# Loading all gate and value weights in the first gate step, and placing a finished block four raw blocks back

## The chip, the cores and the metric

The kernel runs on one core of a Trainium2 chip. The metric is the time of one launch in device microseconds, as the median of repeated runs. One more execution was taken under the hardware profiler, and all rows below come from it.

## The reference, cut to what matters

```python
# q, k, v: (8 batches, 8 heads, 576, 64), fp32
k_p = k.reshape(B, H, 72, 8, 64).mean(axis=3); v_p = likewise
scores = (q @ k_p.T) / 8;  attn = softmax(scores);  o = attn @ v_p
x = o.transpose(0, 2, 1, 3).reshape(4608, 512)
h = (sigmoid(x @ w_gate) * (x @ w_val)) @ w_out       # 512 -> 1536 -> 512
y = (h @ w_in); out = (y * cos(y)) @ w2_out           # 512 -> 2048 -> 512
```

The weights come as eight-byte doubles (the kernel reads them as pairs of 32-bit words), everything else as fp32.

## The kernel before, in words

The 4608 rows are worked through in nine chunks of 512 rows. Attention, the two gate products and the first half of the second layer are interleaved so that TensorE always has the next product to run. A chunk c of the gate stage has twelve gate steps f = 0 to 11. A gate step multiplies the chunk's xT (a high and a low fp32r part) by one 128-column block of w_gate and one of w_val (`gv_step`, L591; three products for each of four k-blocks, 24 matmuls, L601 to L603). ScalarE then takes the sigmoid of the gate product into `g` (L608), VectorE multiplies it by the value product (L609), and a task sent to the next step stores it to DRAM (`gd<-g`, L613). Beside each gate step stand pieces of the next chunk's attention: transposing q (`q_step`, L462/L464), scores and softmax (`s_step`, L475 to L492 and `normal`), transposing the probabilities (`a_step`, L563 to L567), the product with v (`x_step`, L584 to L586), and pooling k and v on GpSimd (L362). In chunk 0 the steps 0 to 2 run as halves of 256 columns, the first halves ahead of the loop.

The weights are converted once, in chunk 0, just ahead of the gate steps that use them. There are 24 blocks, n = 2f for the gate block of step f and n = 2f+1 for its value block. A block goes through five stages:

- a load of 512 KB into a raw tile (`load`, L116, issued on SyncE's queue at L124);
- an exponent stage on ScalarE (`stage_exponent`, L143);
- two bit stages on VectorE (`stage_bits`, L148 and L153);
- the high part on ScalarE (`stage_high`, L161), written to the finished block's own place;
- the low part on VectorE (`stage_low`, through the helper at L66), written to the second half of that place.

`split` (L300) moves this chain on by one round each gate step: first the low parts of blocks whose high part is made, then the high parts of blocks whose bits are done, then exponents of up to four raw blocks that are loaded, then the bits of two. Each engine executes its instructions strictly in this order. A PE matmul of step f needs both parts of blocks 2f and 2f+1.

28 slots w0 to w27 hold both kinds of tile. Finished block n goes to slot n, raw block n to slot n + AHEAD, so block n overwrites raw block n - AHEAD, and its high part waits for the low part of block n - AHEAD, the last reader of that raw tile. From chunk 1 on slots w24 to w27 serve the conversion of the later weights.

SyncE issues every DMA of the kernel, in program order, and waits for whatever the next one needs. Eight raw blocks are loaded before the loop; in the loop each gate step of chunk 0 loads two more at its start (L1243 to L1245), which stand behind the store of the previous step's `g`.

PSUM has two rings of four banks: tag g for gate and value products (two steps deep), tag t for everything of the attention.

Of the kernel before, what the change touches and what calls it, by code (L numbers as in the profile page):

```python
# [23 lines left out]
def attention_two_mlps(  # L24
# [33 lines left out]
    NF = FF // P  # L58
# [46 lines left out]
        "g": (w_gate, True), "v": (w_val, True), "o": (w_out, False),  # L105
        "i2": (w2_in, True), "o2": (w2_out, False),
    }
    AHEAD = 2
    NSLOT = 28
    order = [(kind, f) for f in range(NF) for kind in "gv"]  # L110
    slots = [(wp, f"w{n}") for n in range(NSLOT)]
# [1 line left out]
    raws, blocks = [], {}  # L113
    done = {"exponent": 0, "bits": 0, "high": 0, "parts": 0}

    def load(slot=None, item=None):  # L116

        kind, f = item or order[len(raws)]
        pool, tag = slot or slots[len(raws) + AHEAD]
        t = pool.tile([P, 512], I64, tag=tag, name=f"raw_{kind}{f}")  # L120
        w, columns = sources[kind]
        c = slice(f * P, (f + 1) * P)
        if columns:
            nc.sync.dma_start(  # L124
                t.rearrange("p (kb c) -> p kb c", kb=KB), w[:, c].rearrange("(kb p) c -> p kb c", p=P)
            )
        else:
            nc.sync.dma_start(t, w[c, :])
        if item is None:
            raws.append(t)  # L130
        return t

    def load_all():
        while len(raws) < min(len(order), len(slots) - AHEAD):
            load()
# [38 lines left out]
    def far_stores():  # L174
        while ready:
            nc.sync.dma_start(*ready.pop(0))
# [83 lines left out]
    def i2_weights(hold):  # L260

        made = {}

        def begin(n, j):
            raw = hold[:, n % 4]
            nc.sync.dma_start(
                raw.rearrange("p (kb c) -> p kb c", kb=KB),
                w2_in[:, j * P:(j + 1) * P].rearrange("(kb p) c -> p kb c", p=P),
            )

        def convert(n):
            stage_exponent(hold[:, n % 4])
            stage_bits([hold[:, n % 4]])

        def high(n, j):
            tag = free_i2.pop(0)
            t = wp.tile([P, 2, DM], F32R, tag=tag, name=f"wi2{j}")
            nc.scalar.copy(t[:, 0], words(hold[:, n % 4], F32, 1))
            made[j] = t
            place["i2", j] = wp, tag  # L280

        def low(n, j):
            t = made.pop(j)
            split_lo(nc.vector, t[:, 1], words(hold[:, n % 4], F32, 1), t[:, 0])
            blocks["i2", j] = t

        events = {}
        for n, j in enumerate(PAIRED):
            at = n if n < 4 else 11 + 5 * (n - 4) // 4
            for later, fn, args in (  # L290
                (4, low, (n, j)), (0, begin, (n, j)), (2, convert, (n,)), (3, high, (n, j)),
            ):
                events.setdefault(at + later, []).append((fn, args))
        order_ = {low: 0, high: 1, convert: 2, begin: 3}
        for n in range(max(events) + 1):
            for fn, args in sorted(events.get(n, ()), key=lambda e: order_[e[0]]):
                fn(*args)
            yield

    def split(upto=None, n=2):  # L300

        upto = len(raws) if upto is None else upto
        while done["parts"] < done["high"]:
            stage_low(done["parts"])
            done["parts"] += 1
        while done["high"] < done["bits"]:
            stage_high(done["high"])
            done["high"] += 1
        while done["exponent"] < min(done["bits"] + 2 * n, upto):
            stage_exponent(done["exponent"])  # L310
            done["exponent"] += 1
        some = range(done["bits"], min(done["bits"] + n, done["exponent"]))
        stage_bits(some)
        done["bits"] += len(some)
# [3 lines left out]
    def refill(tag):  # L318
        if not refills:
            free_i2.append(tag)  # L320
            return
        kind, j = refills.pop(0)
        t = wp.tile([P, 2, DM], F32R, tag=tag, name=f"w{kind}{j}")
        nc.sync.dma_start(t.bitcast(F32), wd[kind, j])
        blocks[kind, j] = t
        place[kind, j] = wp, tag
# [264 lines left out]
    def gv_step(c, f, half=None):  # L591
        cols = slice(0, C) if half is None else slice(half * C // 2, (half + 1) * C // 2)
        n = cols.stop - cols.start
        x = xT[c][..., cols]
        pg = []
        for kind in "gv":
            w = block(kind, f)
            p = bank("g", [P, n], f"p{kind}{c}_{f}_{cols.start}")
            for kb in range(KB):
                wh, wl = (w[:, n, kb * P:(kb + 1) * P] for n in range(2))  # L600
                nc.tensor.matmul(p, wh, x[:, 0, kb], start=kb == 0, stop=False)  # L601
                nc.tensor.matmul(p, wh, x[:, 1, kb], start=False, stop=False)  # L602
                nc.tensor.matmul(p, wl, x[:, 0, kb], start=False, stop=kb == KB - 1)  # L603
            pg.append(p)
        g = halves.pop(f, None)
        if g is None:
            g = gv.tile([P, C], F32, tag="g", name=f"g{c}_{f}", bufs=4)
        nc.scalar.activation(g[:, cols], pg[0], AF.Sigmoid)  # L608
        nc.vector.tensor_tensor(out=g[:, cols], in0=pg[1], in1=g[:, cols], op=ALU.mult)  # L609
        if half == 0:  # L610
            halves[f] = g
        elif c == 0:
            afterwards(1, lambda: nc.sync.dma_start(gd[f], g))  # L613
        elif f < HF:
            firsts[c, f] = g
            afterwards(1, lambda: nc.sync.dma_start(od[c][0, :, f], g[:, :HALF]))
        else:
            folded(c, f - HF, firsts.pop((c, f - HF)), g)
# [8 lines left out]
    def tick():  # L627
        clock[0] += 1
        for fn in tasks.pop((clock[0], False), ()):
            fn()  # L630

    def tock():
        for fn in tasks.pop((clock[0], True), ()):
            fn()
# [492 lines left out]
    with tc.manual_schedule():  # L1127
# [84 lines left out]
        def far_step():  # L1212
            far_stores()
            next(far, None)

        plans = [plan(c) for c in range(1, NC)]
        for c in range(NC):
            last = c == NC - 1
            beside = [[] for _ in range(NF)]
            if not last:  # L1220
                steps, early = plans[c]
                for n in range(NF):
                    if c == 0:
                        beside[n] += early[n]
                    beside[n] += steps[n]
                    if c + 1 < NC - 1:
                        beside[n] += plans[c + 1][1][n]
            else:
                far_stores()
                for _ in far:  # L1230
                    far_stores()
                far_stores()
                free_i2.extend(f"w{n}" for n in range(2 * NF, NSLOT))
                at.release()
                mp = tc.alloc_tile_pool(name="mp", bufs=1, side="left", reuse_waits="tile")
                i2 = i2_weights(
                    mp.tile([P, 4, 512], I64, tag="x2", name="raw_i2", bufs=2)
                )
                pp[0] = tc.alloc_tile_pool(name="pp1", bufs=1, side="left", reuse_waits="tile")
            for at_f, f in enumerate(FOLDED if c else range(NF)):  # L1240
                tick()
                if c == 0:
                    for _ in range(2):  # L1243
                        if len(raws) < 2 * NF:
                            load()  # L1245
                    split()
                elif last:
                    if at_f == NF - 1:
                        pp[0].release()
                        pp[0] = tc.alloc_tile_pool(  # L1250
                            name="pp2", bufs=1, side="left", reuse_waits="tile"
                        )
                    (unit_go if at_f == NF - 1 else go.go)()
                    next(i2)
                else:
                    split()
                    far_step()
                gv_step(c, f, 1 if c == 0 and f < FIRST else None)
                if last:
                    for kind in "gv":  # L1260
                        refill(place[kind, f][1])
                    next(i2)
                    for n in range((0, 0, 0, 1, 1, 1, 2, 2, 2, 2, 1, 0)[at_f]):
                        if n:
                            go.go()
                        o_next()
                    if at_f == NF - 1:
                        unit_go()
                elif c:
                    far_step()  # L1270
                for step in beside[at_f]:
                    step()
                tock()
        while tasks:
            tick()
# [107 lines left out]
```

## Time and profile before

| | |
|---|---|
| median of 3 runs | 1812.24 us (1810.19 to 1814.11) |
| the profiled execution | 1815.71 us, its span 1813.9 us |
| PE busy | 1759.1 us, 97% of the span |
| DVE busy | 1117.2 us, 62% |
| ACT busy | 913.9 us, 50% |
| DMA, mean | 219 GB/s |

The page cuts the span into 40 slices of 45 us. PE is the busy engine in nearly all of them; the exceptions lie at the start. A wait of another engine costs time only where PE runs dry because of it. Windows give, for a stretch, the busy time of each engine, the granted TensorE clock (1.00 is 2.4 GHz, 0.50 is 1.2 GHz) and the share of DMA time.

### The profile page before, as it was taken

The numbers are of one execution on the slowest core, as the hardware profiler recorded it, in microseconds if no ns is written. First come the engines' busy times: TensorE is split into PE (matmuls) and PEld (weight loads), VectorE is DVE, ScalarE is ACT, GpSimd is POOL, SyncE is SP. The second block draws the span as 40 slices with busy tenths as digits, with TensorE's granted clock in tenths as the row PEclk, the third lists the DMA queues.
The fourth block names the chain that finished last, engine by engine and source line by source line (L and its number), as shares of the span: only waits on it lengthen the run. The fifth ranks groups of instructions, "written<-read, shape, count | busy, mean of one in ns | idle before, by whom it ended". The sixth has DMA issues, their size and how long they took to land. (4 is left out here: it accounts for less than half of the span.)

```text
span 1813.9 us, 24656 instructions
## 1 busy us (share of the span) xinstructions
PE 1759.1 (97%) x8560; PEld 1474.6 (81%) x8560; DVE 1117.2 (62%) x1830; ACT 913.9 (50%) x1528; POOL 535.4 (30%) x656
## 2 busy tenths in 40 slices
PE   5879999999999999998999999999999999999999
PEld 4768888888888888886888888888887878888887
DVE  7675656546565655345666776776676665565665
ACT  6463544445454444335555555555555554444443
POOL 4102454644454422210003333443334440000000
PEclk8889999999999999999999999999999999999999
DMA  8434475666556754957877778778738798666664
GB/s 235 143 104 139 146 222 177 223 187 191 174 194 211 225 186 164 367 191 232 280 261 259 255 245 263 253 251 260 259 131 275 239 323 277 211 218 217 210 218 148
DMA packets 291741, 397.49 MB, mean 219 GB/s; under 512 B 54560, under 2 KB 231200, under 8 KB 291616
## 3 DMA queue, kind: packets, MB, share of 16 engines
q1 hardware_dynamic: 291616, 395.91, 67.0%
q8 instruction: 68, 1.11, 0.3%
q14 instruction: 57, 0.47, 0.1%
HBM read 242.22 MB, written 153.62 MB: 218 GB/s over the span
## 5 line engine op out<-in xcount | busy, mean ns | idle before, releaser
L609 DVE TENSOR_TENSOR g<-pv,g 128x512 f32<-128x512 f32 (+1 forms) x111 | 75.0, 676 | 280.7 <-issue 130.4
L904 PE MATMUL ph<-x,wi 128*128 128x512 f32 x576 | 224.5, 390 | 0.4 <-DVE r L920 0.4
L905 PE MATMUL ph<-x,wi 128*128 128x512 f32 x576 | 224.2, 389 | 0.0
L906 PE MATMUL ph<-x,wi 128*128 128x512 f32 x576 | 224.1, 389 | 0.0
L910 DVE SCALAR_TENSOR_TENSOR r<-n,ph 128x512 f32<-128x512 int32 x144 | 98.8, 686 | 198.4 <-issue 91.3
L916 ACT ACTIVATE r<-r 128x512 f32<-128x512 f32 x144 | 91.1, 633 | 237.2 <-DVE r L913 107.2
L938 POOL TENSOR_TENSOR s<-r,r 128x256 f32<-128x256 f32 x64 | 75.2, 1175 | 442.4 <-DVE r L920 324.3
L601 PE MATMUL pg<-xT,wg 128*128 128x512 f32 (+1 forms) x444 | 180.5, 406 | 2.3 <-ACT e L519 2.3
L66 DVE TENSOR_TENSOR sp<-sf,sp 128x1024 fp32r<-128x1024 f32 x112 | 132.7, 1227 | 81.0 <-ACT sp L994 81.0
L603 PE MATMUL pg<-xT,wg 128*128 128x512 f32 (+1 forms) x444 | 173.6, 391 | 1.1 <-DVE wg L66 1.1
L602 PE MATMUL pg<-xT,wg 128*128 128x512 f32 (+1 forms) x444 | 173.4, 391 | 0.1
L603 PE MATMUL pv<-xT,wv 128*128 128x512 f32 (+1 forms) x444 | 171.1, 385 | 0.0
L601 PE MATMUL pv<-xT,wv 128*128 128x512 f32 (+1 forms) x444 | 171.1, 385 | 0.0
L602 PE MATMUL pv<-xT,wv 128*128 128x512 f32 (+1 forms) x444 | 171.0, 385 | 0.0
L994 ACT CAST sp<-sf 128x1024 fp32r<-128x1024 f32 x112 | 112.4, 1055 | 67.6 <-PE py_B L1097 25.0
L608 ACT ACTIVATE g<-pg 128x512 f32<-128x512 f32 (+1 forms) x111 | 65.2, 587 | 135.7 <-PE pg L603 83.5
L904 PEld LDWEIGHTS ph<-x,wi 128*128 128x128 f32 x576 | 108.4, 188 | 23.6 <-DVE r L920 1.1
L905 PEld LDWEIGHTS ph<-x,wi 128*128 128x128 f32 x576 | 108.3, 188 | 22.6
L906 PEld LDWEIGHTS ph<-x,wi 128*128 128x128 f32 x576 | 108.2, 188 | 22.5
L1092 PE MATMUL py_A<-tc,sp 128*128 128x512 f32 x384 | 120.6, 395 | 0.0
L913 DVE SCALAR_TENSOR_TENSOR r<-n,r 128x512 f32<-128x512 int32 x144 | 108.3, 752 | 5.0
L66 DVE TENSOR_TENSOR up<-uf,up 128x1024 fp32r<-128x1024 f32 x84 | 102.3, 1218 | 5.4 <-ACT up L818 5.4
(178 smaller groups left out, 4086.0 us busy)
## 6 DMA issues: line engine op xcount, KB each, us to landing
sf<-sd SPq DMA_DIRECT2D x112, 512.0 KB
so<-so SPq DMA_DIRECT2D x84, 512.0 KB
uf<-od SPq DMA_DIRECT2D x168, 256.0 KB
sd<-s SPq DMA_DIRECT2D x64, 512.0 KB
wo<-wo SPq DMA_DIRECT2D x56, 512.0 KB
od<-tg SPq DMA_DIRECT2D x48, 512.0 KB
sd<-r SPq DMA_DIRECT2D x64, 256.0 KB
raw_o<-in_moe_w_out_dram SPq DMA_DIRECT2D x28, 512.0 KB
```

Source lines behind the costliest of these rows:

```text
L66: engine.tensor_tensor(out=lo, in0=x, in1=hi.bitcast(F32), op=ALU.subtract)
L601: nc.tensor.matmul(p, wh, x[:, 0, kb], start=kb == 0, stop=False)
L602: nc.tensor.matmul(p, wh, x[:, 1, kb], start=False, stop=False)
L603: nc.tensor.matmul(p, wl, x[:, 0, kb], start=False, stop=kb == KB - 1)
L904: nc.tensor.matmul(p, wh, x[kb][:, 0], start=kb == 0, stop=False)
L905: nc.tensor.matmul(p, wh, x[kb][:, 1], start=False, stop=False)
L906: nc.tensor.matmul(p, wl, x[kb][:, 0], start=False, stop=kb == KB - 1)
L910: nc.vector.scalar_tensor_tensor(out=r, in0=n, scalar=-C1, in1=p, op0=ALU.mult, op1=ALU.add)
L913: nc.vector.scalar_tensor_tensor(out=r, in0=n, scalar=-C2, in1=r, op0=ALU.mult, op1=ALU.add)
L916: nc.scalar.activation(r, r, AF.Sin, scale=0.5)
L994: nc.scalar.copy(t[:, 0, h * w:(h + 1) * w], got[c, n, h])
L1092: nc.tensor.matmul(p, x[:, 0, m, s], w, start=fresh and m == 0, stop=False, skip_group_check=True,)
```

## The change

Two edits. AHEAD becomes 4: raw block n goes to slot n + 4 and finished block n takes the place of raw block n - 4 (slots w4 to w27 for the 24 raw blocks, all of them fresh). And the two loads at the start of each gate step of chunk 0 go; instead `load_all` issues all that are missing, sixteen, at the end of gate step 0.

```diff
-    AHEAD = 2
+    AHEAD = 4
...
                 if c == 0:
-                    for _ in range(2):
-                        if len(raws) < 2 * NF:
-                            load()
                     split()
...
                 for step in beside[at_f]:
                     step()
+                if c == 0 and at_f == 0:
+                    load_all()
                 tock()
```

`load_all` (L133) loads until `min(len(order), len(slots) - AHEAD)` = 24 blocks are there. As `split` looks at how many blocks are loaded, the conversions move too: step 0 finds no ninth and tenth block, and from step 1 on each round works on blocks two numbers lower than before.

On SyncE's queue, from the last load of the next chunk's keys to the store of step 2. Before:

```order
L380 DMA raw_k_2_655<-in_k_dram 64x1x512
L613 DMA gd<-g_0_463 128x512
L124 DMA raw_g_665<-in_moe_w_gate_dram 128x4x128
L124 DMA raw_v_667<-in_moe_w_val_dram 128x4x128
L613 DMA gd<-g_1_517 128x512
L124 DMA raw_g_741<-in_moe_w_gate_dram 128x4x128
L124 DMA raw_v_743<-in_moe_w_val_dram 128x4x128
L454 DMA q_256_785<-in_q_dram 128x8x64
L613 DMA gd<-g_2_600 128x512
```

The same place now, from the end of the batch of sixteen:

```order
L124 DMA raw_v_680<-in_moe_w_val_dram 128x4x128
L124 DMA raw_g_682<-in_moe_w_gate_dram 128x4x128
L124 DMA raw_v_684<-in_moe_w_val_dram 128x4x128
L613 DMA gd<-g_0_463 128x512
L613 DMA gd<-g_1_517 128x512
L454 DMA q_256_795<-in_q_dram 128x8x64
L613 DMA gd<-g_2_600 128x512
```

The loads moved ahead of the first store; behind it no weight load is left.

On ScalarE, gate steps 1 and 2 (wg, wv with L161 are high parts, raw with L143 exponents). Before:

```order
L161 CAST wg_669<-raw_g_603 128x512
L161 CAST wv_671<-raw_v_605 128x512
L143 ACTIVATE raw_g_665<-raw_g_665 128x512
L143 ACTIVATE raw_v_667<-raw_v_667 128x512
L608 ACTIVATE g_1_517<-pg_1_256_679 128x256
L487 ACT_TABLE_LOAD
L487 ACTIVATE e_512_718<-e_512_718 64x288 x2
L161 CAST wg_747<-raw_g_665 128x512
L161 CAST wv_749<-raw_v_667 128x512
```

And now:

```order
L143 ACTIVATE raw_g_654<-raw_g_654 128x512
L143 ACTIVATE raw_v_656<-raw_v_656 128x512
L143 ACTIVATE raw_g_658<-raw_g_658 128x512
L143 ACTIVATE raw_v_660<-raw_v_660 128x512
L608 ACTIVATE g_1_517<-pg_1_256_695 128x256
L487 ACT_TABLE_LOAD
L487 ACTIVATE e_512_734<-e_512_734 64x288 x2
L161 CAST wg_757<-raw_g_654 128x512
L161 CAST wv_759<-raw_v_656 128x512
```

Step 1 now makes four exponents (blocks 8 to 11) and no high part; the high parts of blocks 8 and 9 came in step 1 and come in step 2.

On VectorE, around the product of step 8, the low parts of the blocks that gate step 10 reads (n = 20, 21). Before (wg_1165, wv_1167):

```order
L430 TENSOR_TENSOR vr<-vRp_1215,mask 128x512
L66 TENSOR_TENSOR wg_1165<-raw_g_1079,wg_1165 128x512
L66 TENSOR_TENSOR wv_1167<-raw_v_1081,wv_1167 128x512
L609 TENSOR_TENSOR g_8_1257<-pv_8_0_1244,g_8_1257 128x512
L480 TENSOR_REDUCE mx_384_1261<-psc_384_0_1262 64x4
L481 TENSOR_TENSOR e_384_1260<-psc_384_0_1262,mx_384_1261 64x288
```

And now (wg_1217, wv_1219):

```order
L491 TENSOR_REDUCE sm_384_1268<-e_384_1254 64x4 x2
L529 TENSOR_SCALAR sm_384_1268<-sm_384_1268 64x8
L532 RECIPROCAL sm_384_1268<-sm_384_1268 64x8
L535 TENSOR_TENSOR a_384_1273<-e_384_1254,sm_384_1268 64x512
L540 TENSOR_TENSOR a_384_1273<-e_384_1254,sm_384_1268 64x4x2x32
L66 TENSOR_TENSOR aT_1_1062<-pa_256_1276,aT_1_1062 128x4x128
L66 TENSOR_TENSOR aR_1_1063<-par_256_1277,aR_1_1063 64x2x128
L66 TENSOR_TENSOR wg_1217<-raw_g_678,wg_1217 128x512
L66 TENSOR_TENSOR wv_1219<-raw_v_680,wv_1219 128x512
L609 TENSOR_TENSOR g_9_1321<-pv_9_0_1308,g_9_1321 128x512
```

They stood ahead of step 8's product and softmax; now they stand behind them, one gate step before their use instead of two.

## Rows read from the trace of the kernel before

**Rows 1.** The page, 40 slices of the span: PE busy tenths.
```profile
PE   5879999999999999998999999999999999999999
```

**Rows 2.** Waits of PE from 56 to 160 us: total, times, longest.
```profile
PE px L584 <- ACT qT L464: 6.8, 1, 6.8
PE px L584 <- DVE e L481: 3.6, 2, 3.4
PE psc L475 <- DVE kbd L413: 3.4, 1, 3.4
PE pq L462 <- issue: 1.3, 1, 1.3
PE psc L475 <- ACT qT L464: 1.1, 1, 1.1
```

**Rows 3.** Windows: length, then busy us of each engine, clock, DMA share, GB/s.
```profile
80.00:90.00 10.00, 8.89 (x41) 6.91 (x39) 6.00 (x12) 5.55 (x11) 3.46 (x4) 0.83 1.03 297
100.00:110.00 10.00, 2.95 (x14) 2.72 (x15) 7.24 (x18) 6.08 (x13) 0.00 (x0) 0.52 0.42 136
110.00:120.00 10.00, 10.00 (x47) 8.56 (x46) 6.45 (x13) 5.33 (x10) 0.00 (x0) 0.79 0.41 135
```

**Rows 4.** Waits of ACT from 50 to 131 us.
```profile
ACT wg L161 <- DVE wg L66: 17.2, 7, 4.2
...
ACT raw_g L143 <- DMA raw_g<-in_moe_w_gate_dram: 4.5, 2, 3.3
...
ACT raw_v L143 <- DMA raw_v<-in_moe_w_val_dram: 2.4, 2, 1.7
```

**Rows 5.** Timeline of SyncE's queue: start, us, then the DMAs issued.
```profile
23.05 1.41 SPq L124 DMA_DIRECT2D raw_g<-in_moe_w_gate_dram  x1
...
35.50 0.63 SPq L380 DMA_DIRECT2D raw_k<-in_k_dram  x1
61.10 0.43 SPq L124 DMA_DIRECT2D raw_g<-in_moe_w_gate_dram  x1
```

**Rows 6.** Windows, columns as above.
```profile
44.00:60.00 16.00, 11.92 (x68) 11.42 (x68) 11.26 (x22) 5.93 (x12) 2.43 (x4) 0.68 0.01 1
67.00:111.00 44.00, 27.77 (x137) 22.87 (x136) 32.51 (x71) 25.26 (x43) 7.78 (x9) 0.84 0.56 165
111.00:142.00 31.00, 31.00 (x145) 25.34 (x145) 24.25 (x52) 19.57 (x35) 0.00 (x0) 0.95 0.32 102
```

**Rows 7.** Waits of DVE from 67 to 142 us.
```profile
DVE raw_v L148 <- DMA raw_v<-in_moe_w_val_dram: 3.1, 3, 1.9
DVE raw_g L148 <- DMA raw_g<-in_moe_w_gate_dram: 1.9, 1, 1.9
...
DVE aT L66 <- ACT aT L564: 1.1, 1, 1.1
DVE xT L66 <- ACT xT L585: 0.8, 1, 0.8
DVE sm L491 <- ACT e L487: 0.5, 3, 0.2
```

**Rows 8.** Timeline of PE: the first matmul of gate step 10, and of x behind step 11.
```profile
138.46 0.39 PE L601 MATMUL pg<-xT,wg 128*128 128x512 f32 x1
...
150.10 0.57 PE L584 MATMUL px<-aT,vm 128*128 128x448 f32 x2
```

**Rows 9.** Windows behind a PE wait of 1.20 us at 186.9 us.
```profile
190.00:192.00 2.00, 2.00 (x6) 1.56 (x5) 0.23 (x1) 0.00 (x0) 1.92 (x3) 0.50 0.46 186
```

**Rows 10.** Timeline of DVE: the same operation beside GpSimd's adds, and without.
```profile
90.55 1.07 DVE L535 TENSOR_TENSOR a<-e,sm 128x512 f32<-128x512 f32 x1
...
102.15 0.69 DVE L535 TENSOR_TENSOR a<-e,sm 128x512 f32<-128x512 f32 x1
```

**Rows 11.** Timeline of ACT: the sigmoids of gate steps 4 and 5.
```profile
97.68 0.60 ACT L608 ACTIVATE g<-pg 128x512 f32<-128x512 f32 x1
...
107.58 0.60 ACT L608 ACTIVATE g<-pg 128x512 f32<-128x512 f32 x1
```

## The prediction, made before the changed kernel was run

> **What bounds the kernel now.** I read the page's 40 slices first. PE stands at 9 nearly everywhere; below that are the first three slices of 45 us and one in the middle [rows 1]. So a gain must come out of the first 135 us or so, and any time that PE saves there is kept, since PE goes on without a gap that this change touches. Next I read PE's own waits in the stretch that the change can reach, from the loop's first step at 56 us to the end of chunk 0. Five waits stand there: 6.8, 3.6, 3.4, 1.3 and 1.1 us, 16.2 us together [rows 2]. PE's clock falls as well: behind the three long waits the granted clock is 0.83, 0.52 and 0.79 in windows of 10 us [rows 3]. A mean of 0.83 is 34% of the time at the lower of two levels, 1.2 GHz. Half of the busy time spent there is lost: 0.34 x 8.89 / 2 = 1.5 us, 0.96 x 2.95 / 2 = 1.4 us, 0.42 x 10 / 2 = 2.1 us, 5.0 us in all. So 16.2 + 5.0 = 21.2 us is the ceiling of what the change can give there.
>
> Then I looked at what the releasers were doing. PE waits for ScalarE's and VectorE's softmax pieces, and these engines wait for the weights: ScalarE 17.2 us in seven waits for a low part on VectorE, the wait that AHEAD sets, and 4.5 + 2.4 us for the loads [rows 4]. VectorE itself waits 3.1 + 1.9 us for loads [rows 7]. The loads are late because they are issued late: from 36 to 61 us SyncE issues nothing, as the next two loads stand behind the store of step 0's product [rows 5], and the DMA share is 0.01 meanwhile [rows 6].
>
> **The change, part by part.** *Sixteen loads in step 0.* They now stand behind the last key load, which SyncE issues at 35.5 us [rows 5]; two loads ahead of it are gone, at 1.4 us each, so the batch starts at about 33 us. At 1.4 us for 512 KB sixteen take 22 us: the last is issued near 55 us and lands a few us later, in a stretch where the DMA engines were empty. All their slots are fresh, so none waits. The first is needed in step 1, at about the time of the first load in the loop before (61.1 us), the others two by two in the steps that follow. What stands behind them on SyncE is the store of step 0's product, ready just before 61 us and needed by nobody soon; were the loads twice as slow, the batch would end at 78 us and delay the stores and the load of a q tile, which only step 5 reads. I cost the loads at nothing, covered by the empty DMA window; all waits for loads go: 6.9 us on ScalarE, 5.0 on VectorE, partly the same time. The keys of the next chunk land up to 3 us earlier and GpSimd pools them earlier; what that shifts before 56 us I cost at zero, between -1 and +1 us.
>
> *AHEAD = 4.* A high part now waits for a low part four blocks back, made a round earlier, so the 17.2 us of ScalarE's waits go. What is late next? Each step was a hand-over: low part on VectorE, high part, exponents, sigmoid on ScalarE, product and softmax on VectorE, low part. With the wait gone ScalarE reaches its sigmoid while VectorE is still at the softmax of the step before, and VectorE's own work sets the pace. It is not small: from 67 to 142 us it is busy 32.51 + 24.25 = 56.8 us of 75 [rows 6].
>
> *The conversions a round later.* This is the part that costs. VectorE must have made the low parts of step 10's blocks before PE starts step 10; before, these stood ahead of step 8's softmax, now behind it and ahead of step 9's product. So the start of step 10 on PE is VectorE's time from 67 us. Its work up to there is the 56.8 us less 1.2 us (the low parts of step 11's blocks, now behind this point) less about 1.0 us by which it is further along at 67 us (it has the product of step 1 and the start of a softmax done, but not yet the bits of blocks 10 and 11): 54.6 us. Waits that stay are those inside the chains from a PE product over ScalarE to VectorE: 1.1 + 0.8 + 0.5 = 2.4 us [rows 7]. Step 10 then starts at 67 + 54.6 + 2.4 = 124.0 us instead of 138.5 us [rows 8], a gain of 14.5 us. From there to the x products behind step 11 PE has the same 11.6 us as before [rows 8].
>
> PE itself, at the full clock and without waits, would reach step 10 at 138.5 - 21.2 = 117.3 us; so it waits some 6.7 us for VectorE in steps 3 to 10, in several pieces. These can lower its clock: behind a wait of 1.20 us later on, a window of 2 us has a granted clock of 0.50 [rows 9]. The loss at the lower clock is hidden where PE waits for VectorE anyway, except behind the last wait, the one ahead of step 10. I take one such loss, 1.7 us, the nearest measured (0.83 in the first window above, 1.5 us, is much the same), between 0 and 5 us. The sum is 14.5 - 1.7 = 12.8 us.
>
> The uncertain term is what VectorE still waits for. Its waits between 67 and 142 us are 75 - 56.8 = 18.2 us; 5.0 of them are the loads. If none stays the gain is 12.8 + 2.4 = 15.2 us, without the clock loss 16.9 us; if all but the loads' stay, 13.2 instead of 2.4, it is 12.8 - 10.8 = 2.0 us. I take 2.4 because the largest of the others follow from ScalarE's lateness, which goes.
>
> Beside GpSimd's adds a VectorE multiplication takes 1.07 us, without them 0.69 us [rows 10]. This is in the 32.51 us already, since the values are pooled in that stretch, before and after. The Trainium skill, SBUF — State Buffer, section "Who interferes with whom", says that a VectorE instruction with two SBUF inputs and a GpSimd instruction that reads SBUF exclude each other, so that one stands for the whole instruction of the other. By that rule the pooling could cost more now that VectorE seldom idles; this is the second rival below.
>
> The profiled execution is 1815.71 us, 1.8 us of it outside the span, and 3.5 us above the median of the runs. 1815.7 - 12.8 = 1802.9 us for such an execution; against the median, 1812.24 - 12.8 = 1799.4 us.
>
> **The rivals.** *Only the loads count.* The hand-over between ScalarE and VectorE keeps its pace because softmax, not the slot, holds it: ScalarE waits for VectorE's scores anyway, only then takes exponents and sigmoid. For it: the sigmoids of steps 4 and 5 are 9.9 us apart [rows 11] though neither waits for a load. Against it: the 17.2 us are the largest of ScalarE's waits. The gain is VectorE's 5.0 us of loads, 1807 us.
>
> *GpSimd in VectorE's way.* The value pooling, 7.78 us between 67 and 111 us [rows 6], falls into a stretch in which VectorE has no idle time. If VectorE stood for all of it, beyond the slowing that is already in its rows, up to 7 us would be added to its chain: a gain of 6 us, 1806 us. Against it: the operations slowed so far lost 0.4 us each.
>
> *Slower: PE waits for its weights in each step.* The low parts are made one step ahead instead of two, behind softmax. If a step still takes VectorE and ScalarE 9.9 us [rows 11], steps 3 to 9 from 67 us on bring step 10 to 67 + 7 x 9.9 = 136.3 us, 2.2 us earlier than before, and PE now waits just ahead of each weight block; four such waits with 1.7 us of lower clock that nothing hides make 6.8 us: 4.6 us slower, 1817 us. It decides when a step's VectorE work is over about 9 us; the rows have 56.8 us for seven and a half steps, 7.6 us.
>
> *The change does little.* The waits shift into each other and the clock loss comes at each of them (up to 5 us beside a gain of 5): 1811 us.
>
> *More.* VectorE waits for nothing and step 10 is not late: 17 to 20 us, 1794 us.
>
> **How the numbers follow.** Forecast 55%, only the loads 13%, GpSimd 10%, slower 4%, little 10%, more 8%. The forecast's own range is a gain of 8 to 16.9 us, 1795 to 1804 us. For 8 in 10 the range takes in the two middle rivals: 1794 to 1808 us. About 0.2%, 3.6 us, is what a measurement can tell. Faster needs less than 1808.6 us: the forecast, "more", GpSimd and most of "only the loads", 0.85; same 0.11; slower 0.04.
>
> **What would show it.** In the changed profile: SyncE issues sixteen weight loads in a row between 33 and 60 us with a full DMA share; no wait of ScalarE or VectorE for raw_g or raw_v behind 56 us; the wait of L161 for the low part (17.2 us) gone or under 3 us; PE waits of 16.2 us down to 5 to 8 us, with a new one for a wg block (L66) ahead of step 9 or 10; the x products behind step 11 at about 137 us instead of 150.1; behind that the same distances as before. It is wrong if L161's waits are gone and PE's are not, or if the time comes back behind 150 us.

## The result, and the profile after

The changed kernel takes 1792.82 us (median of 5 runs, 1792.21 to 1797.18), the kernel before beside it 1811.4 us: a ratio of 0.990, 95% interval 0.9888 to 0.9911, or 18.1 us (16.1 to 20.3). On a second chip it was 1795.87 against 1812.58 us, a ratio of 0.9906 (0.989 to 0.9922), 17.0 us. Forecast were 1799.4 us, 12.8 us of gain, with a range that ends at 1794 us; the measured 1792.82 us lies 1.2 us below that end. The direction was right, and so was the mechanism in the loop; the gain was larger, for reasons that the last part takes apart.

The waits of PE from 56 to 160 us in the changed kernel, against the five of [rows 2] (us in total, times, longest):

```profile
PE px L584 <- ACT qT L464: 3.3, 1, 3.3
PE pg L603 <- DVE wg L66: 1.0, 1, 1.0
```

16.2 us became 4.3 us, where 5 to 8 were forecast, and the new one is the wait that was forecast, for a low part. On PE's timeline stand, in this order, the loop's step 0, step 10, the wait inside step 10, and the x products behind step 11:

```profile
53.14 0.28 PE L601 MATMUL pg<-xT,wg 128*128 128x256 f32 x1
...
119.28 0.39 PE L601 MATMUL pg<-xT,wg 128*128 128x512 f32 x1
...
120.86 0.50 PE L603 MATMUL pg<-xT,wg 128*128 128x512 f32 x1 [0.96 <-DVE wg L66]
...
132.18 0.78 PE L584 MATMUL px<-aT,vm 128*128 128x448 f32 x3
```

Step 10 stood at 138.46 us, the x products at 150.10 us [rows 8]. Step 0 stood here in the kernel before:

```profile
56.57 0.28 PE L601 MATMUL pg<-xT,wg 128*128 128x256 f32 x1
```

So three stretches can be told apart: up to step 0 (56.6 before, 53.1 now), from step 0 to the x products, called the loop below (93.5 before, 79.0 now), and from there to the end of the span (1663.8 and 1658.2). The table below lists them for every run, since the rest of this document is about which of them an edit moves.

The loads are where they were expected. The rows show the first of sixteen, the last, and the stores behind them (start, us):

```profile
32.92 0.44 SPq L124 DMA_DIRECT2D raw_g<-in_moe_w_gate_dram  x1
...
54.45 1.42 SPq L124 DMA_DIRECT2D raw_v<-in_moe_w_val_dram  x1
56.74 3.78 SPq L613 DMA_DIRECT2D gd<-g  x2
```

ScalarE's largest waits from 50 to 131 us, which answer to [rows 4], no longer name a weight tile:

```profile
ACT e L487 <- DVE e L481: 14.1, 10, 4.2
ACT g L608 <- PE pg L603: 10.7, 5, 2.6
```

What ScalarE waits for now is VectorE's softmax, and VectorE is busy: 52.39 of 57.7 us in a window from the end of step 2 to step 10 (columns as in [rows 3]; the same shares in [rows 6] were 32.51 of 44 and 24.25 of 31):

```profile
63.30:121.00 57.70, 53.26 (x269) 44.14 (x268) 52.39 (x115) 41.04 (x73) 8.17 (x9) 0.94 0.22 65
```

PE's clock still falls once, behind the wait of 3.3 us at 86 us:

```profile
80.00:90.00 10.00, 6.66 (x39) 5.69 (x37) 9.65 (x22) 6.09 (x13) 0.83 (x2) 0.88 0.07 26
90.00:100.00 10.00, 9.86 (x45) 8.48 (x45) 6.54 (x16) 5.24 (x9) 0.00 (x0) 0.78 0.07 27
```

### The profile page after: what moved, and what is told of

It reads as the page before. It is cut to its first block, busy times and chain, and to the rows that moved or that the text cites. A ratio compares the mean times of both kernels' runs of the same rounds, so it can differ in the third digit from the quotient of the medians.

```text
span 1790.4 us, 24638 instructions
## 1 busy us (share of the span) xinstructions
PE 1750.6 (98%) x8560; PEld 1468.4 (82%) x8560; DVE 1115.6 (62%) x1830; ACT 912.4 (51%) x1528; POOL 534.2 (30%) x656
## 5 line engine op out<-in xcount | busy, mean ns | idle before, releaser
L609 DVE TENSOR_TENSOR g<-pv,g 128x512 f32<-128x512 f32 (+1 forms) x111 | 75.1, 676 | 274.7 <-issue 135.4
L603 PE MATMUL pg<-xT,wg 128*128 128x512 f32 (+1 forms) x444 | 172.3, 388 | 3.0 <-DVE wg L66 3.0
L603 PE MATMUL pv<-xT,wv 128*128 128x512 f32 (+1 forms) x444 | 170.9, 385 | 0.0
L994 ACT CAST sp<-sf 128x1024 fp32r<-128x1024 f32 x112 | 112.5, 1056 | 67.1 <-PE py_B L1097 25.0
```

The source lines that it names most:

```text
L994: nc.scalar.copy(t[:, 0, h * w:(h + 1) * w], got[c, n, h])
```

## The experiments

Times are medians; ratios are against runs of the kernel before on the same chip. The three stretches are from one profile each, read on PE's timeline. One more point is listed, *block*: the time at which PE takes up the first product that needs the low part of step 2's gate block (L603), in the first half of step 2 that runs just ahead of step 0.

| kernel | median us | ratio (95%) | block at | step 0 at | step 0 to x | x to end |
|---|---|---|---|---|---|---|
| before | 1811.4 | | 52.1 | 56.6 | 93.5 | 1663.8 |
| before, second profile | (1813.1) | | 52.6 | 57.0 | 93.3 | 1661.0 |
| changed | 1792.8 | 0.990 (0.9888 to 0.9911) | 50.4 | 53.1 | 79.0 | 1658.2 |
| changed, again | 1795.9 | 0.9906 (0.989 to 0.9922) | 50.3 | 54.7 | 78.5 | 1665.2 |
| e1 AHEAD alone | 1810.0 | 0.9983 (0.9974 to 0.9993) | 52.7 | 55.4 | 89.8 | 1660.3 |
| e2 loads alone | 1804.3 | 0.9953 (0.994 to 0.9966) | 50.4 | 54.1 | 85.9 | 1660.1 |
| e3 pair first | 1798.5 | 0.9925 (0.9911 to 0.9939) | 52.8 | 55.5 | 79.6 | 1659.4 |
| e4 pair behind the keys | 1813.0 | 0.9996 (0.9987 to 1.0005) | 51.2 | 55.7 | 94.0 | 1660.0 |
| e5 key sums short | 1809.1 | 0.9977 (0.9966 to 0.9987) | 49.4 | 52.1 | 93.5 | 1660.3 |
| e6 extra round | 1796.8 | 0.9911 (0.9897 to 0.9926) | 50.7 | 55.3 | 80.6 | 1662.9 |
| e7 extra round, lows first | 1797.8 | 0.9913 (0.9898 to 0.9928) | 49.4 | 52.9 | 81.5 | 1660.9 |
| e8 lows first | 1794.3 | 0.9893 (0.9879 to 0.9908) | 48.8 | 51.6 | 79.0 | 1661.9 |
| e9 changed, key sums short | 1795.5 | 0.9908 (0.989 to 0.9925) | 49.0 | 51.7 | 80.0 | 1659.6 |
| e10 changed, value sums short | 1792.8 | 0.9886 (0.9869 to 0.9902) | 50.7 | 55.2 | 75.1 | 1661.9 |

The theory behind the first four (P): the loop's gain needs both edits, and what step 0 gains comes from the pair of weight loads that no longer stands ahead of the keys. The rival (Q): it comes from ScalarE's high parts, which no longer wait.

**e1, AHEAD = 4 alone.**

```diff
-    AHEAD = 2
+    AHEAD = 4
```

> AHEAD = 4 alone, loads two by two as before. Theory P (the 3.4 us that step 0 starts earlier in the changed kernel come from the pair of weight loads that no longer stands ahead of the next chunk's keys): step 0 starts within 0.5 us of before (56.6 us), as the pair is still there. Rival Q (they come from ScalarE's high parts that no longer wait): step 0 starts at about 53 us. On the loop both agree: ScalarE's wait for the low parts (17.2 us) is gone, its waits for loads (6.9 us) stay or grow; the whole gains 2 to 9 us, 1803 to 1810 us, clearly less than the full change.

The loop gained 3.7 us of 14.5, at the low end of what was expected. ScalarE's wait for the low parts is gone, but its waits for loads grew from 6.9 us [rows 4] to 17.3:

```profile
ACT raw_g L143 <- DMA raw_g<-in_moe_w_gate_dram: 11.1, 7, 3.5
...
ACT raw_v L143 <- DMA raw_v<-in_moe_w_val_dram: 6.2, 7, 1.4
```

The one wait stood in front of the other. Step 0 came 1.2 us earlier, between what P and Q said.

**e2, the sixteen loads alone.** The changed kernel with AHEAD = 2.

> All sixteen loads at the end of step 0, AHEAD = 2. Theory P: step 0 starts at about 53 us as in the changed kernel, the pair being gone. Rival Q: at 56.6 us as before. Loop: no wait for loads, but ScalarE's wait for the low parts stays (some 15 us) and the conversions are a round later, so PE waits 2 to 5 us for a low part ahead of step 10: 4 us gained in the loop, with P 1803 to 1805 us, with Q 1806 to 1808 us.

Right on the loop, which gained more than expected, 7.7 us. ScalarE waits for no load any more; the other wait is now the one that stays, 20.1 us where [rows 4] had 17.2:

```profile
ACT wg L161 <- DVE wg L66: 20.1, 8, 4.0
```

Alone the two edits gain 3.7 and 7.7 us in the loop, together 14.5, more than the sum of the two. Step 0 came 2.5 us earlier, between P and Q again.

**e3, the pair ahead of the keys, in the changed kernel.**

```diff
                 if c == 0:
+                    if at_f == 0:
+                        load()
+                        load()
                     split()
```

> The changed kernel, but blocks 8 and 9 are loaded at the start of step 0, as before, ahead of the keys; the other fourteen at its end. The conversions are therefore back at their old rounds. Theory P: step 0 starts at 56.6 us as before, the 3.4 us are lost; the wait ahead of step 10 (0.96 us) is gone; the loop from step 0 on is as long as in the changed kernel or up to 1.5 us shorter: 1795 to 1797 us. Rival Q: step 0 starts at 53 us, 1792 us or less.

The loop took 79.6 us: the conversions a round earlier again are worth nothing. Step 0 lost 2.4 of the 3.4 us, by the first profile of the changed kernel, 0.8 by the second. The whole, 1798.5 us, is longer than the 1795 to 1797 of P.

**e4, the pair behind the keys, in the kernel before.** Its two loads of step 0 moved to the step's end.

> The kernel before with one edit: the pair of loads of step 0 (blocks 8 and 9) stands at the step's end, behind the keys; all others as before, AHEAD = 2. Theory P: step 0 starts at about 53 us, and GpSimd's key sums start at 35.5 instead of 38.4 us. Rival Q: step 0 starts at 56.6 us. In the loop the conversions run a round later with loads still late: -2 to +2 us. P: 1806 to 1811 us; Q: 1810 to 1813 us.

GpSimd's key sums started at 36.1 us, earlier as P said, but step 0 came only 0.9 us earlier, not 3.4, and the whole stayed as it was (1813.0 us). Read at step 0, P fails as it stood, and with e1 so does Q: neither edit alone moves step 0 by the whole. The column *block* says more. The waits that end there, before and in the changed kernel:

```profile
52.11 0.58 PE L603 MATMUL pg<-xT,wg 128*128 128x256 f32 x1 [1.09 <-DVE wg L66]
```

```profile
50.41 0.39 PE L603 MATMUL pg<-xT,wg 128*128 128x256 f32 x1 [2.00 <-DVE wg L66]
```

With the pair of loads ahead of the keys (both profiles of the kernel before, e1, e3) PE gets there at 52.1 to 52.8 us; with it behind them (both profiles of the changed kernel, e2, e4, e6, e10) at 50.3 to 51.2 us, with AHEAD at 2 or at 4. So up to this point P holds and Q fails. From there to step 0 PE only multiplies, without a wait, and takes 2.7 us at a granted clock of 1.00 (the changed kernel's first profile, e1, e3), 4.4 to 4.5 us at 0.55 to 0.57 (its second profile, both of the kernel before, e4, e6, e10) or 3.6 us at 0.72 (e2). This clock follows neither edit. The time of step 0 mixes the two.

Left to explain was why the place of the pair moves the block, and so what VectorE does there. Its four bit operations on blocks 4 and 5, in the kernel before (start, us):

```profile
41.54 1.49 DVE L148 TENSOR_SCALAR raw_g<-raw_g 128x512 int32<-128x512 int32 x1
42.95 0.94 DVE L148 TENSOR_SCALAR raw_v<-raw_v 128x512 int32<-128x512 int32 x1
43.81 0.94 DVE L153 SCALAR_TENSOR_TENSOR raw_g<-raw_g 128x512 int32<-128x512 int32 x1
44.67 1.21 DVE L153 SCALAR_TENSOR_TENSOR raw_v<-raw_v 128x512 int32<-128x512 int32 x1
```

And in the changed kernel:

```profile
42.44 0.68 DVE L148 TENSOR_SCALAR raw_g<-raw_g 128x512 int32<-128x512 int32 x1
43.05 0.55 DVE L148 TENSOR_SCALAR raw_v<-raw_v 128x512 int32<-128x512 int32 x1
43.51 0.68 DVE L153 SCALAR_TENSOR_TENSOR raw_g<-raw_g 128x512 int32<-128x512 int32 x1
44.11 0.68 DVE L153 SCALAR_TENSOR_TENSOR raw_v<-raw_v 128x512 int32<-128x512 int32 x1
```

GpSimd's key sums start at 38.35 us before and at 35.51 us now, when their data land, and end 3 us earlier. Theory G: they are what slows VectorE there. The 2.0 us are not the whole account: the sums now stand beside a softmax piece ahead of these operations, and PE waits 3.0 us for it (`a`, L535), where its longest wait of the kind was 0.8 us before.

**e5, the kernel before with one of three rounds of the key sums.**

```diff
-        for w in (4, 2, 1):
+        for w in ((1,) if short else (4, 2, 1)):
...
```

`short` is true for the keys of batch 1 alone; the lines that pass it on are left out here.

> The kernel before, but GpSimd adds only one of the three rounds of sums for the keys of batch 1 (left out: six of the eight key rows of each pool of that batch). Theory G (what holds the stretch ahead of step 0 is VectorE slowed beside GpSimd's key sums): VectorE's bit operations at 41.5 us take 0.43 and 0.69 us instead of 1.49, 0.94, 0.94 and 1.21, PE's wait of 4.2 us for the low part of the probabilities shrinks by about 2 us, and step 0 starts at 53 to 54.5 us instead of 56.6. Rival C (it is PE's clock in step 2's first half, which falls or not by small shifts): the VectorE operations are shorter, but step 0 moves by less than 1.5 us or by what the clock of step 2's first half (6.2 us at the lower, 4.4 us at the higher level) says.

The operations took 0.42, 0.42, 0.81 and 0.68 us, PE's wait for the low part of the probabilities fell from 4.2 to 1.9 us, and step 0 came at 52.1 us, 4.5 us earlier than before and earlier than G said. Of these 4.5 us, 2.7 stand at the block (49.4 us against 52.1); the other 1.7 us are PE's clock behind it (2.7 us to step 0 instead of 4.5), the second branch of C. So G holds for the 2.7 us, more than C alone allows.

```profile
41.20 0.42 DVE L148 TENSOR_SCALAR raw_g<-raw_g 128x512 int32<-128x512 int32 x1
41.53 0.42 DVE L148 TENSOR_SCALAR raw_v<-raw_v 128x512 int32<-128x512 int32 x1
41.87 0.81 DVE L153 SCALAR_TENSOR_TENSOR raw_g<-raw_g 128x512 int32<-128x512 int32 x1
42.59 0.68 DVE L153 SCALAR_TENSOR_TENSOR raw_v<-raw_v 128x512 int32<-128x512 int32 x1
```

**e9, the same edit in the changed kernel.**

> The changed kernel with GpSimd adding only one of three rounds of the key sums of batch 1 (the others are left out). Theory G: in the changed kernel the sums fall on other, less urgent VectorE operations, but still slow them (1.59 instead of 0.69 us for one multiplication); without them step 0 starts at 50.5 to 52 us, 1.5 to 2.5 us faster than the changed kernel, less than the 3.7 us that the same edit gave the kernel before. Rival: the overlap no longer matters, within 1 us.

Step 0 at 51.7 us, against 52.1 in e5, and the block at 49.0 against 49.4, both behind it at the full clock: without most of the key sums the change is worth 0.4 us ahead of step 0, with them 1.7 to 2.3 us at the block. So it is mainly through GpSimd's sums that the change reaches that stretch. For the whole the rival's branch came: nothing gained that can be told from the changed kernel (1795.5 against 1795.9 us).

**The kernel before again, and the changed one again.**

> The kernel before once more, for a second profile of it. If the clock of step 2's first half and the wait of 1.2 us at 187 us belong to the kernel, both stand here again: step 0 at 56.6 us, the x products behind step 11 at 150 us, 1664 us from there to the end of the span. If they are of one execution: step 0 anywhere from 54.5 to 57 us, and about 1660 us behind, as in the four runs so far.

> The changed kernel once more, for a second profile and for a comparison on one chip with the two below. If the 3.4 us ahead of step 0 belong to the change: step 0 at 53 to 53.5 us, x products behind step 11 at 132 us, ratio to before near 0.990. If part of them is where PE's clock happened to fall: step 0 anywhere between 53 and 55.5 us, the stretch from step 0 to the x products 79 us all the same, ratio up to 0.992.

Both kernels keep the loop's length to 0.6 us (93.5 and 93.3, 79.0 and 78.5). Step 0 stays at 56.6 and 57.0 before, but moves from 53.1 to 54.7 in the changed kernel; e6 and e10, which have the same program up to there, give 55.3 and 55.2. The granted clock differs: in the window from 50 to 57 us it is 1.00 in the first profile of the changed kernel and 0.71 in the second (0.57 and 0.54 in the two of the kernel before):

```profile
50.00:57.00 7.00, 6.59 (x54) 6.39 (x55) 3.29 (x8) 1.16 (x4) 0.00 (x0) 1.00 1.10 348
```

```profile
50.00:57.00 7.00, 6.67 (x42) 6.67 (x43) 2.50 (x5) 0.92 (x3) 0.00 (x0) 0.71 1.10 348
```

At the block the first profiles differ by 1.7 us and the second ones by 2.3 us: that much belongs to the change. The other 1.7 us of the 3.4 are the clock between the block and step 0, full in one execution of the changed kernel and lower in the other, as in both of the kernel before:

```profile
50.41:53.14 2.73, 2.73 (x22) 2.73 (x23) 0.55 (x1) 0.38 (x1) 0.00 (x0) 1.00 1.10 348
```

```profile
50.33:54.72 4.39, 4.39 (x23) 4.39 (x23) 0.55 (x1) 0.38 (x1) 0.00 (x0) 0.57 1.10 348
```

The wait of 1.2 us at 187 us [rows 9] does not come again in the second profile of the kernel before: it belonged to one execution. And the last stretch, 1658.2 and 1665.2 us for one and the same program, varies by more than it differs between the kernels; the 5.6 us that the first two profiles differ by there cannot be put down to the change.

**e6, an extra conversion round behind the sixteen loads.** A call of `split()` behind `load_all()`.

> The changed kernel with one more conversion round at the end of step 0, behind the sixteen loads, so that every low part is made a round earlier again. If lateness of the low parts costs time: the wait ahead of step 10 (0.96 us) goes and with it some of VectorE's queue, 1 to 2 us faster than the changed kernel, 1791 to 1793 us. If VectorE's total work sets the loop (as e3 suggests, whose loop was 79.6 us against 79.0): no difference, the wait turns up ahead of the x products of step 5, 1793 to 1795 us.

The wait ahead of step 10 is gone and the loop is no shorter, 80.6 us; PE's wait ahead of the x products of step 5 grew from 3.3 to 4.4 us. The second branch holds, though the whole, 1796.8 us, is longer than it said: lateness of the low parts is not what the loop loses.

**e7, as e6, with the low parts of blocks 4 and 5 ahead of those of x**, and **e8, that order without the extra round.**

```diff
         split()
+        split()
         for i in range(KB):
             x_step(0, 1, i, 1)
-        split()
         gv_step(0, 2, 0)
```

> As the one before, and the low parts of blocks 4 and 5 stand ahead of the low parts of x on VectorE, just before the loop. In the changed kernel PE waits 2.0 us there for the low part of step 2's gate block. If that wait is what remains ahead of the loop: gone, step 0 starts 1.5 to 2 us earlier, 1 to 2 us faster than the kernel before it in this list. Rival: x's low parts, now later, are waited for instead at step 0: no difference.

> The changed kernel with the low parts of blocks 4 and 5 ahead of those of x on VectorE just before the loop, without the extra conversion round. The wait of 2.0 us for step 2's gate block goes; step 0 starts 1 to 2 us earlier than in the changed kernel on the same chip, the loop stays at 79 us: 1 to 2 us faster. If PE's clock covers it: within 1 us.

Step 0 came at 52.9 and 51.6 us, and the block at 49.4 and 48.8, as the wait of 2.0 us is gone in e7 and 0.5 in e8. e7 loses it again in its longer loop, 81.5 us: it was expected to be faster than e6 and is not (1797.8 against 1796.8 us). e8 has the best median of its chip, 1794.3 us against 1795.9 of the changed kernel; with intervals that overlap this is not shown to be faster.

**e10, the changed kernel with one of three rounds of the value sums.** The edit of e5, for the values.

> The changed kernel with GpSimd adding only one of three rounds of the value sums of batch 1 (the others are left out). In the changed kernel these sums slow four VectorE operations of steps 3 and 4 (1.52, 0.96, 0.69 and 0.81 us where 0.42, 0.43, 0.42 and 0.69 stand without them), 2.0 us together. If VectorE's work sets the pace of the loop: the stretch from step 0 to the x products behind step 11 falls from 79.0 and 78.5 us to 75 to 77.5 us, PE's wait of 3.3 us ahead of the x products of step 5 to 2 us or less. Rival (the hand-over with ScalarE, or PE itself, sets it): 78 to 79 us.

The loop fell to 75.1 us, 3.4 to 4.0 us shorter, though only some 2 us of VectorE's time were taken away (63.25 us busy in the changed kernel's loop, 60.91 here). PE's wait fell to 1.1 us, and as it did, the clock stayed up (0.88 and 0.78 above):

```profile
PE px L584 <- ACT qT L464: 1.1, 1, 1.1
```

```profile
80.00:90.00 10.00, 8.92 (x53) 7.69 (x51) 9.65 (x22) 8.18 (x15) 0.00 (x0) 1.00 0.07 26
90.00:100.00 10.00, 9.46 (x52) 8.18 (x52) 7.96 (x20) 6.08 (x12) 0.00 (x0) 1.00 0.14 54
```

VectorE's work sets the pace of the loop now, what GpSimd's sums add to it included. The ratio of the whole, 0.9886, has an interval that overlaps with the changed kernel's.

## Why the prediction was right in kind and too small

*The ceiling and where it lies.* Right: the loop gained 14.5 us by the first profiles and 14.8 by the second, out of a ceiling of 21.2. Nothing is seen to come back behind it, but the last stretch differs by 7 us between executions, so a loss of a few us there could not be seen.

*Loads at no cost.* Right: issued from 32.9 to 55.9 us, no wait for a load behind 56 us. The rival "only the loads" is out by e2, since AHEAD adds 6.8 us to the loop on top of them.

*AHEAD and VectorE as the next bound.* Right, and shown by e10. e1 and e2 add what the prediction did not say: the two waits stood one in front of the other, so that neither edit alone gets its share.

*Step 10 at VectorE's pace.* Right in the sum, in part by luck. The low part that step 10 waits for was forecast for 124.0 us, 67.4 us behind step 0; it was ready 67.7 us behind step 0 in the first profile and 67.1 us in the second. But in the first profile's window that answers to the forecast's (63.57 to 120.80 us) VectorE works 51.95 us where 54.6 were taken, and waits 5.3 us where 2.4 were taken: the two errors cancel. Step 10 itself begins earlier than its low part is there (119.28 us, with the wait at its third product): only the third product of a k-block reads the low part, L603. That every matmul of a step needs both parts, as the description of the kernel has it, is too strict. The window (63.57 is the 67 us of the forecast less the 3.4 us by which step 0 is earlier):

```profile
63.57:120.80 57.23, 52.85 (x266) 43.73 (x264) 51.95 (x114) 40.72 (x73) 8.17 (x9) 0.94 0.22 64
```

*A clock loss of 1.7 us behind the last wait.* This term was mis-sized: no such loss is seen. Behind the wait ahead of the third product PE runs at full clock, and the x products follow after 11.32 us in both profiles, where 11.6 + 1.7 = 13.3 us were taken:

```profile
121.00:132.20 11.20, 11.20 (x53) 8.98 (x54) 3.71 (x7) 1.74 (x4) 3.37 (x4) 1.00 0.64 166
```

The 1.7 us answer to the wait of [rows 9]: half of 3.4 us at the lower clock in three windows of 2 us behind it, of which the rows show the middle one. The two beside it:

```profile
188.00:190.00 2.00, 2.00 (x14) 1.77 (x13) 1.53 (x6) 1.37 (x4) 1.84 (x5) 0.80 0.19 66
192.00:194.00 2.00, 2.00 (x9) 1.61 (x8) 0.00 (x0) 0.52 (x1) 0.33 (x1) 0.85 0.55 198
```

That wait did not come again in the second profile of the same kernel. This term is most of why the loop gained 14.5 us and not the 12.8 of the sum.

*"What that shifts before 56 us I cost at zero, between -1 and +1 us."* This is the step that failed. I saw that the keys land 3 us earlier and that GpSimd slows VectorE (1.07 for 0.69 us, [rows 10]), but put the second only into the loop. Ahead of step 0 VectorE's bit operations beside the key sums cost 4.58 us before and 2.59 now, and PE waits at the end of that chain. At the block PE is 1.7 us earlier by the first two profiles and 2.3 by the second; e1 to e4 show that this follows the place of the pair of loads, e5 and e9 that it comes through GpSimd's sums. At step 0 itself the two profiles give 3.4 and 2.3 us, the first with 1.7 us of PE's clock in it. What set that clock stays open: it was full or lower with the pair on either side of the keys. With 14.5 and 14.8 us in the loop that makes 17.9 and 17.1 us, near what the ratios of the medians show (18.1 and 17.0).

*The rivals.* "GpSimd in VectorE's way" named a true cost, 3.4 to 4.0 us of the loop by e10, but it was in VectorE's rows already: VectorE is busy 63.9 us in the loop before and 63.3 us in the changed kernel, so the change added nothing to it. Of the slower rival's waits for a weight block there is one in the loop, of 0.96 us. From the sigmoid of step 3 to that of step 10 a step now takes 7.8 us on average, though steps 4 and 5 alone are still 10.1 us apart:

```profile
69.12 0.61 ACT L608 ACTIVATE g<-pg 128x512 f32<-128x512 f32 x1
...
78.38 0.60 ACT L608 ACTIVATE g<-pg 128x512 f32<-128x512 f32 x1
...
88.50 0.60 ACT L608 ACTIVATE g<-pg 128x512 f32<-128x512 f32 x1
...
123.46 0.60 ACT L608 ACTIVATE g<-pg 128x512 f32<-128x512 f32 x1 [2.61 <-PE pg L603]
```

The gain came out in the range of "More", 17 to 20 us, but not for its reason: VectorE waits, and the low part of step 10 is late.

The rule cited from the Trainium skill, SBUF — State Buffer, section "Who interferes with whom", is about VectorE operations with two SBUF inputs, and the trace agrees that GpSimd's sums slow these: L153, which reads both words, takes 0.94 and 1.21 us beside them and 0.68 us behind their end. Whether one stands for the whole instruction of the other no row here shows. The larger slowing, 1.49 for 0.42 us, is that of L148, which has one SBUF input and which the cited rule does not cover. I read the slowing as a cost only; it made a gain where the sums moved away from an urgent operation.

## What to carry to other kernels

When a transfer moves, follow what it wakes on every engine, also those that nothing waits for: here GpSimd's sums moved 3 us and VectorE's urgent work beside them got 2 us shorter. When two waits alternate on one engine, try both edits together; each alone shows a fraction (3.7 and 7.7 of 14.5 us). A gain of a few us ahead of a loop has to be read from two profiles, since a second execution of the same program moved it by 1.6 us; better still at a wait that ends ahead of where the clock differs, here the block, which moved by 0.1 us (by 0.5 us in the kernel before).

## What was not expected of the hardware

One VectorE operation beside GpSimd's sums took 1.49 us instead of 0.42, over three times as long. Removing some 2 us of such slowing gained 3.4 to 4.0 us; PE's wait shrank by 2.2 us, and behind it PE's clock no longer fell (granted 1.00 and 1.00 instead of 0.88 and 0.78), which may be the rest but was not tested by itself. The same 22 products of step 2's first half took 2.73 us in one execution of the changed kernel and 4.39 us in another (granted clock 1.00 and 0.57). The last 1660 us of one program, in which PE is almost always busy, differed by 7 us between two executions.
